# New planned durations and priorities for the attention part of an attention and two-MoE kernel

## The chip, the cores and the metric

The kernel runs on one core of a Trainium2 chip. The metric is the device time of one execution in microseconds (us); three runs of the kernel before gave 1052.19, 1050.07 and 1051.02, median 1051.02 us. PE is TensorE, DVE is VectorE, ACT is ScalarE, POOL is GpSimd and SP is the engine that issues the DMAs here.

## The reference

Inputs are q, k, v of shape (4, 8, 576, 64), a memory M of (4, 8, 64, 64) with a normaliser z of (4, 8, 64), and one gate beta per head. Per head:

```
local = softmax(causal(q k^T / 8)) v
q_p   = phi(q)                  # phi(x) = x + 1 for x > 0, else exp(x)
mem   = (q_p M) / (q_p . z + 1e-6)
out   = g mem + (1 - g) local   # g = sigmoid(beta)
```

The result, seen as 2304 tokens of 512 values, goes through two feed-forward layers (512 to 2048 to 512): `(mish(x w_in)) w_out`, and then the same with silu and a second pair of weights. The weights arrive as 64-bit floats.

## The kernel before, in words

**Attention.** The 32 heads are done as 16 pairs; a pair's two heads stand side by side in the 128 partitions. The operations of one pair are listed with their planned engine, duration and dependencies in `pair_steps()`. Their names: `ld*` loads; `phe`, `phu`, `phf` make phi(q) (two halves on ACT, the joining on DVE), `phz`, `phr`, `pha`, `phd`, `phg`, `phm` its normalised form (POOL and DVE); `Tk`, `Tq`, `Tp`, `Ts`, `Tr` are PE transposes and `Tkh`, `Tqh`, ... their copies out of PSUM (`Ts` and `Tr` are the 64-row remainder; `Tsqh` and `Tsph` are two small copies each on DVE, `Tph` two on ACT). For query blocks 4 to 0: scores `s` on PE, masking with the row extreme `r` on DVE, exponential with row sum `e` on ACT, then `a` (POOL), `d` (DVE, reciprocal) and the normalisation `n` (POOL). `X1` to `X6` and `Xs` transpose the normalised probabilities on PE, `X1h` and so on copy them to the tiles h and W (odd numbers on ACT, even ones on DVE; `X1h` and `X5h` are three copies), `Vhi` and `Vlo` multiply by V and M on PE, and `Vhic`, `Vloc` copy the result to xT.

**Weights.** Each of the 64 jobs of a weight block (two layers, 16 blocks, two parts) is loaded, decoded from 64-bit to 32-bit floats in five DVE steps (`abs`, `b0` to `b3`, lines 757 to 772), rounded on ACT (`hi`, line 780), and the rest is formed on POOL (`lo`, line 784). Eight jobs fit in beside attention; two more can be decoded and then wait. There are two raw buffers and one for the value.

**MoE.** Tokens come in six blocks of 384, the 2048 inner values in four groups of four blocks. A unit is `in` (12 matmuls, lines 838 to 840), the activation and its split (lines 853 to 855), and `out` (matmuls of line 875). Its input is split into xh and xl (lines 821 and 824). The steps `open0` and `open1` swap the memory of attention's "early" and "late" pools for that of the MoE: `open0` waits for the loads, phi, T, s, r and e steps of the last two pairs, and xh waits for it; the first `out` waits for `open1`, which needs the rest of attention.

**What sets the order.** A planner (`Steps.plan`) replays all operations with their planned durations on five engines, with ring buffers counted; an engine that is free takes, of the operations that are ready, the one with the smallest `late`. That is the due time less the longest planned way to it; pairs fall due one PERIOD apart, and a table SHIFT then adds a number to `late` for every kind of operation (key `('a', name)` for all pairs, `('W', step)` for all weight jobs, `('x', 'h')` and `('x', 'l')` for the input split of the first MoE):

```
for k, x in self.shift.items():
    late[k] += x
```

The order in which the replay starts the operations is the order in which they are written to the engines' queues; the hardware runs each queue in that order, with semaphores between. So a planned duration or a shift has no effect on any instruction, only on the order. The planner's `act(n)` is 0.051 + n/1200 us, `dve(n)` 0.066 + n/960.

Of the kernel before, what the change touches and what calls it, by code (L numbers as in the profile page):

```python
# [202 lines left out]
P = 128  # L203
B, H, S, D = 4, 8, 576, 64
# [7 lines left out]
def width(i):  # L212
    return ST + P * i


def mm(n, k=1):
    return k * max(0.109, n / 2215)


def act(n, ps=True, ptr=0):  # L220
    return (0.051 if ps else 0.093) + n / 1200 + 0.093 * ptr


def dve(n):
    return 0.066 + n / 960
# [26 lines left out]
def pair_steps():  # L252
    m = Pair()
    E = m.place
    for nm, d in (("nk", 1.6), ("nq", 1.7), ("nv", 3.1)):
        E("ld" + nm, "S", d, [], 2.7)
    E("phe", "A", act(640, False), ["ldnq"])
    E("phu", "A", act(640, False), ["ldnq"])
    m.group("t", ("Tk", "P", 0.44, ["ldnk"]), [("Tkh", "A", act(512), ["Tk"])])
    E("phf", "D", dve(640), ["phe", "phu"])  # L260
    m.group("t", ("Tq", "P", 0.44, ["ldnq"]), [("Tqh", "D", dve(512), ["Tq"])])
    E("phz", "G", 1.5, ["phf"])
    E("phr", "D", dve(640), ["phz"])
    E("pha", "G", 0.297, ["phr"])
    E("phd", "D", 0.13, ["pha"])
    E("phg", "G", 0.17, ["phd"])
    E("phm", "G", 1.23, ["phg"])
    m.group("t", ("Ts", "P", 0.11, ["ldnk", "ldnq"]),
            [("Tskh", "A", act(128), ["Ts"]), ("Tsqh", "D", 0.27, ["Ts"])])
    m.group("t", ("Tr", "P", 0.06, ["phm"]),  # L270
            [("Tsph", "D", 0.27, ["Tr"])])
    qk = ["Tkh", "Tqh", "Tskh", "Tsqh"]
    for i in (4, 3, 2, 1):
        for x in range(2 if i == 4 else 1):
            n = SA if i == 4 else width(i)
            E(f"s4{x}" if i == 4 else f"s{i}", "P", mm(n, 4), qk)
        for j in range(2):
            w = width(i)
            if i == 4:
                for x in range(2):  # L280
                    E(f"r4{j}{x}", "D", dve(SA) + 0.067 * x, [f"s4{x}"] + ([f"r4{j}0"] if x else []), 0.17)
                    m.uses.append(("s", f"s4{x}{j}", [f"s4{x}"], [f"r4{j}{x}"]))
                dep = [f"r4{j}1"]
            else:
                E(f"r{i}{j}", "D", dve(w), [f"s{i}"], 0.17)
                m.uses.append(("s", f"s{i}{j}", [f"s{i}"], [f"r{i}{j}"]))
                dep = [f"r{i}{j}"]
            E(f"e{i}{j}", "A", act(w, False, 2), dep)
            r = f"r4{j}0" if i == 4 else f"r{i}{j}"
            m.uses.append(("sm", r, [r], [f"e{i}{j}"]))  # L290
        E(f"a{i}", "G", 0.273, [f"e{i}0", f"e{i}1"])
        E(f"d{i}", "D", 0.08, [f"a{i}"])
        for j in range(2):
            E(f"n{i}{j}", "G", 0.327 + width(i) / 1200, [f"d{i}"])
        if i == 3:
            m.group("t", ("Tp", "P", 0.44, ["phm"]), [("Tph", "A", 2 * act(512), ["Tp"])])
        if i == 1:
            m.group("s", ("s0", "P", 0.25, qk), [("r00", "D", dve(ST), ["s0"], 0.17)])
            E("e00", "A", act(ST, False, 2), ["r00"])
            m.uses.append(("sm", "r00", ["r00"], ["e00"]))  # L300
            E("a0", "G", 0.273, ["e00"])
            E("d0", "D", 0.08, ["a0"])
            E("n00", "G", 0.434, ["d0"])

        def X(g, deps):
            m.group("t", (f"X{g}", "P", 0.44, deps),
                    [(f"X{g}h", "A", 3 * act(256) if g in (1, 5) else act(512), [f"X{g}"]) if g % 2 else (f"X{g}h", "D", dve(512), [f"X{g}"])])

        def V(half, groups):
            w = S - HI0 if half == "hi" else HI0  # L310
            n = f"V{half}"
            m.group("x", (n, "P", 1.99 if half == "hi" else 1.29, ["Tph", "ldnv", "Tsph"] + [f"X{g}h" for g in groups]),
                    [(n + "c", "A", act(w), [n])])
        if i == 2:
            hi = [f"n{x}{j}" for x in (3, 4) for j in range(2)]
            for g in (1, 2, 3, 4):
                X(g, hi)
            V("hi", (1, 2, 3, 4))
        if i == 1:
            lo = [f"n{x}{j}" for x in (1, 2) for j in range(2)]  # L320
            X(5, lo)
            m.group("t", ("Xs", "P", 0.11, ["n00"]), [("Xsh", "D", 0.45, ["Xs"])])
            X(6, lo)
            V("lo", (5, 6, "s"))
    for n, (e, d, _, _) in m.ops.items():
        if e == "P":
            i = n[1:2]
            m.cols[n] = {
                "s": lambda: (192, 192) if n == "s0" else [3 * (SA if i == "4" else width(int(i)))] * 2,
                "V": lambda: (4608, 4608) if n == "Vhi" else (2816, 2816),  # L330
                "X": lambda: (256, 256) if n == "Xs" else (1024, 1024),
                "T": lambda: (256, 128) if n == "Ts" else (128, 64) if n == "Tr" else (1024, 1024)}[n[0]]()
    return m
# [384 lines left out]
GC = NF // NG  # L718
# [5 lines left out]
class Weights:  # L724
# [64 lines left out]
    def register(self, m, due, last):  # L789

        m.cap.update({"W.raw": 2, "W.val": self.VALS})
        for n, job in enumerate(self.jobs):
            ph, i, part = job
            f = self.steps(n)
            k = i % SLOTS
            ring = f"W.{k}{part}"
            m.cap[ring] = 1
            J = lambda x: ("W", job, x)
            t = due(job)
            for x, e, d, deps in (("ld", "S", 3.8, []), ("abs", "D", 0.465, ["ld"]), ("b0", "D", 0.465, ["abs"]),  # L800
                                  ("b1", "D", 0.465, ["b0"]), ("b2", "D", 0.735, ["b1"]), ("b3", "D", 0.78, ["b2"]),
                                  ("hi", "A", 0.57, ["b3"] + (["open1"] if k >= GC else [])),
                                  ("lo", "G", 1.38, ["hi"])):
                m.add(J(x), e, d, [y if y == "open1" else J(y) for y in deps], f[x], t)
            m.hold("W.raw", job, [J("ld")], [J("lo")], order=n)
            m.hold("W.val", job, [J("abs")], [J("b3")], order=n)
            m.hold(ring, job, [J("hi")], last(job), order=n)


class Moe:  # L810
# [185 lines left out]
        self.w.register(m, wdue, wlast)  # L996


PERIOD = 12.53
SHIFT = {  # L1000
# [16 lines left out]
}  # L1017


# [22 lines left out]
def kernel(  # L1042
# [6 lines left out]
    weights = Weights(tc, ctx, [(moe_w_in, moe_w_out), (moe2_w_in, moe2_w_out)])  # L1049
    attn = Attn(tc, xT, q, k, v, M_prev, z_prev, beta, PERIOD)  # L1050
    attn.consts()
# [43 lines left out]
```

## Time and profile before

| | us |
|---|---|
| median of three runs | 1051.02 |
| the profiled execution | 1052.46 |
| its span, first to last instruction | 1050.7 |
| PE busy | 1017.0 (97%), 5824 matmuls |
| DVE busy | 557.5 (53%) |
| ACT busy | 460.2 (44%) |
| POOL busy | 311.1 (30%) |

Busy shares are averages over two unlike parts: attention, up to about 245 us, with all engines at work, and the two MoE layers, in which PE works nearly without a break. Idle time of an engine costs time only where the end hangs on it. An engine's waits are put down to the one that came last. Where one operation starts before the one ahead of it has quite ended, the sum of their durations is a little more than the busy time.

### The profile page before, as it was taken

The page shows a single profiled execution, that of the slowest core. Times are in us where ns is not written, and L with a number is a line of the kernel's source. Part 1 is how long each engine was busy: PE and PEld are TensorE (multiplying, and loading weights), DVE is VectorE, ACT ScalarE, POOL GpSimd, SP SyncE. Part 2 cuts the span into 40 slices and gives each one's busy share as a digit, 9 for nine tenths or more (in the row PEclk, how much of TensorE's full clock was granted, in tenths as well). Part 3 has the DMA queues.
Part 4 walks back from the last instruction along what each step waited for, and adds up shares of the span by engine and source line. Part 5 has one row for each costly group of instructions (what it writes and reads, how often), then busy time and mean ns, then how long its engine had stood idle before and what let it go on. Part 6 is the DMA issues. An engine that isn't in the chain of part 4 may idle for free.

```text
span 1050.7 us, 15745 instructions
## 1 busy us (share of the span) xinstructions
PE 1017.0 (97%) x5824; PEld 903.2 (86%) x5824; DVE 557.5 (53%) x1286; ACT 460.2 (44%) x1071; POOL 311.1 (30%) x413
## 2 busy tenths in 40 slices
PE   6989888989999999999999999999999999999998
PEld 4655555659999999999999999899989999999897
DVE  6999999773743732573278338511752372212222
ACT  6887878887333422332234334423422232222221
POOL 6878897779211200220023325100200120000000
PEclk9999999999999999999999999999999999999999
DMA  5533443200311300220022003200310120000011
GB/s 134 134 91 92 106 103 89 48 14 1 120 42 43 98 21 1 81 81 1 1 82 80 1 3 98 61 1 21 101 40 1 41 81 1 1 1 31 31 61 61
DMA packets 85309, 55.03 MB, mean 52 GB/s; under 512 B 61936, under 2 KB 78320, under 8 KB 85232
## 3 DMA queue, kind: packets, MB, share of 16 engines
q1 hardware_dynamic: 85232, 54.02, 18.2%
q8 instruction: 46, 0.75, 0.3%
q14 instruction: 31, 0.25, 0.1%
HBM read 49.29 MB, written 4.72 MB: 51 GB/s over the span
## 4 chain that ended last, share of the span: by engine, by line
PE 85%; DVE 6%; POOL 4%; ACT 3%; issue 1%; DMA 1%; SPq 0%; POOLq 0%; ACTq 0%; DVEq 0%
PE acc L875 38%; PE hp L838 13%; PE hp L839 13%; PE hp L840 13%; PE ps_s L567 3%; POOL P L599 2%; PE ps_x L672 2%; PE ps_t L636 2%; DVE sm L560 2%; ACT P L584 1%; DVE h L482 1%; ACT W L479 1%; PE ps_t L487 1%; POOL z L614 1%; POOL P L617 0%
## 5 line engine op out<-in xcount | busy, mean ns | idle before, releaser
L853 ACT ACTIVATE a<-hp 128x384 f32<-128x384 f32 x192 | 94.4, 491 | 477.8 <-PE hp L840 477.7
L855 DVE TENSOR_TENSOR gl<-a,gh 128x384 fp32r<-128x384 f32 x192 | 115.4, 602 | 333.3 <-ACT gh L854 333.2
L838 PE MATMUL hp<-xh,w 128*128 128x384 f32 x768 | 259.1, 337 | 0.0
L839 PE MATMUL hp<-xl,w 128*128 128x384 f32 x768 | 258.5, 337 | 0.4 <-POOL xl L824 0.4
L840 PE MATMUL hp<-xh,w 128*128 128x384 f32 x768 | 258.5, 337 | 0.0
L784 POOL TENSOR_TENSOR w<-stg,w 128x512 fp32r<-128x512 f32 x64 | 85.2, 1333 | 471.6 <-ACT w L780 342.8
L875 PE MATMUL acc<-gh,w 128*128 128x384 f32 x768 | 211.8, 337 | 0.0
L875 PE MATMUL acc<-w,gh 128*128 128x512 f32 x576 | 180.4, 394 | 0.0
L839 PEld LDWEIGHTS hp<-xl,w 128*128 128x128 f32 x768 | 144.2, 188 | 4.6 <-POOL xl L824 0.6
L838 PEld LDWEIGHTS hp<-xh,w 128*128 128x128 f32 x768 | 144.2, 188 | 4.5 <-issue 0.3
L840 PEld LDWEIGHTS hp<-xh,w 128*128 128x128 f32 x768 | 144.2, 188 | 0.0
L875 PEld LDWEIGHTS acc<-gh,w 128*128 128x128 f32 x768 | 140.6, 188 | 0.0
L875 PE MATMUL acc<-gl,w 128*128 128x384 f32 x384 | 129.2, 337 | 0.0
L875 PEld LDWEIGHTS acc<-w,gh 128*128 128x128 f32 x576 | 106.9, 188 | 17.4
L892 DVE TENSOR_TENSOR xT<-acc,xT 128x384 f32<-128x384 f32 (+1 forms) x126 | 74.1, 613 | 84.4 <-PE acc L875 84.4
L875 PE MATMUL acc<-w,gl 128*128 128x512 f32 x288 | 113.8, 395 | 0.2 <-DVE gl L855 0.2
L854 ACT CAST gh<-a 128x384 fp32r<-128x384 f32 x192 | 98.6, 514 | 5.9 <-PE acc L875 0.4
L599 POOL TENSOR_SCALAR P<-P,z,g 128x448 f32<-128x448 f32 (+3 forms) x128 | 92.4, 731 | 9.3 <-DVE z L616 7.0
L584 ACT ACTIVATE P<-sm,m 128x448 f32<-128x448 f32 (+4 forms) x144 | 83.4, 582 | 15.1 <-DVE m L560 13.2
L875 PEld LDWEIGHTS acc<-gl,w 128*128 128x128 f32 x384 | 72.1, 188 | 0.0
L636 PE MATMUL ps_t<-ident,P 128*128 128x128 f32 x384 | 57.6, 285 | 9.3 <-POOL P L599 3.7
L636 PEld LDWEIGHTS ps_t<-ident,P 128*128 128x128 f32 x384 | 42.0, 143 | 28.6 <-POOL P L599 7.2
(79 smaller groups left out, 1111.6 us busy)
## 6 DMA issues: line engine op xcount, KB each, us to landing
stg<-in_moe_w_in_dram SPq DMA_DIRECT2D x32, 512.0 KB, 3.7
stg<-in_moe_w_out_dram SPq DMA_DIRECT2D x32, 512.0 KB, 3.5
out_dram<-xT SPq DMA_DIRECT2D x18, 256.0 KB, 2.0
nq<-in_q_dram SPq DMA_DIRECT2D x32, 128.0 KB, 2.7
nk<-in_k_dram SPq DMA_DIRECT2D x32, 128.0 KB, 2.7
nv<-in_v_dram SPq DMA_DIRECT2D x32, 128.0 KB, 2.5
z<-in_z_prev_dram SPq DMA_DIRECT2D x4, 256.0 KB, 4.4
nq<-in_q_dram SPq DMA_DIRECT2D x16, 32.0 KB, 2.5
```

The source lines that it names most:

```text
L584: nc.scalar.activation(G(f"P{i}")[:, 1 - j if i else 1], s[f"sm{i}{j}"], AF.Exp, bias=s[f"m{i}"][:, j:j + 1], scale=-1.0, accum_out=G(f"z{ ...
L599: f[f"n{i}{j}"] = lambda i=i, j=j: nc.gpsimd.tensor_scalar(s[f"P{i}"][:, 1 - j], s[f"P{i}"][:, 1 - j], s[f"z{i}"][:, j:j + 1], self.g1[:, ...
L636: nc.tensor.transpose(ps[:, o:o + P], src, self.ident)
L784: nc.gpsimd.tensor_tensor(w[:, 1, :], self.raw[job][:, :, 0].bitcast(F32), w[:, 0, :].bitcast(F32), op=ALU.subtract)
L838: nc.tensor.matmul(hp, lhsT=wh, rhs=xh, start=(kc == 0), stop=False)
L839: nc.tensor.matmul(hp, lhsT=wh, rhs=xl, start=False, stop=False)
L840: nc.tensor.matmul(hp, lhsT=wl, rhs=xh, start=False, stop=(kc == KC - 1))
L853: f["si"] = lambda: nc.scalar.activation(self.new(u, "a", TB), self.hp[u], fn)
L854: f["gh"] = lambda: nc.scalar.copy(self.new(u, "gh", TB, F32R), g("a"))
L855: f["gl"] = lambda: nc.vector.tensor_tensor(self.new(u, "gl", TB, F32R), g("a"), g("gh").bitcast(F32), op=ALU.subtract)
L875: nc.tensor.matmul(o, lhsT=a, rhs=b, start=(first and k == 0), stop=(last and k == 2))
L892: nc.vector.tensor_tensor(part, acc, part, op=ALU.add)
```

## The change

Planned durations of `phz`, `phg`, `phm`, `Tsqh`, `Tsph`, `Tph`, `X1h`, `X5h`, the normalisations and the five decoding steps of the first eight weight jobs are raised; PERIOD goes from 12.53 to 12.920, and the table SHIFT is replaced (it now also has entries for weights and for xh).

```diff
-    E("phz", "G", 1.5, ["phf"])
+    E("phz", "G", 1.57, ["phf"])
-    E("phg", "G", 0.17, ["phd"])
-    E("phm", "G", 1.23, ["phg"])
+    E("phg", "G", 0.23, ["phd"])
+    E("phm", "G", 1.28, ["phg"])
-            [("Tskh", "A", act(128), ["Ts"]), ("Tsqh", "D", 0.27, ["Ts"])])
+            [("Tskh", "A", act(128), ["Ts"]), ("Tsqh", "D", 0.48, ["Ts"])])
-            [("Tsph", "D", 0.27, ["Tr"])])
+            [("Tsph", "D", 0.48, ["Tr"])])
-            E(f"n{i}{j}", "G", 0.327 + width(i) / 1200, [f"d{i}"])
+            E(f"n{i}{j}", "G", 0.387 + width(i) / 1200, [f"d{i}"])
-            m.group("t", ("Tp", "P", 0.44, ["phm"]), [("Tph", "A", 2 * act(512), ["Tp"])])
+            m.group("t", ("Tp", "P", 0.44, ["phm"]), [("Tph", "A", 1.18, ["Tp"])])
-            E("n00", "G", 0.434, ["d0"])
+            E("n00", "G", 0.5, ["d0"])
-                    [(f"X{g}h", "A", 3 * act(256) if g in (1, 5) else act(512), ...
+                    [(f"X{g}h", "A", 0.91 if g in (1, 5) else act(512), ...
+            slow = 0.2 if ph == 0 and i < GC else 0.0
-                m.add(J(x), e, d, [y if y == "open1" else J(y) for y in deps], f[x], t)
+                m.add(J(x), e, d + (slow if e == "D" else 0.0), [y if y == "open1" else J(y) for y in deps], f[x], t)
-PERIOD = 12.53
+PERIOD = 12.920
```

Entries of SHIFT that the text speaks of, old and new:

```
Tk   18.22   32.27     Tq    7.80   25.99     phu  52.49   63.70
Vhi  47.28  184.28     X3h -13.04 -163.92     X5h  -9.48 -150.25
r401 -0.45 -144.61     r410 -13.59 -153.95    e40  -0.27 -110.98
s3    none  -55.00     Vlo  -6.28  -91.80     x l   2.55   11.88
W ld  none   54.80     W abs none  -30.37     W b0  none  -22.37
W b1  none  -29.57     W b2  none   -3.04     W b3  none   -6.91
W hi  none   -2.90     W lo  none   -9.09     x h   none   -1.87
```

## Rows read from the trace of the kernel before

**Rows 1.** Busy time of each engine by stage; columns in the first line.

```profile
core 0: us, PE busy (x) PEld busy (x) DVE busy (x) ACT busy (x) POOL busy (x), PEclk, DMA share, GB/s
0.00:20.00 20.00, 11.82 (x60) 7.92 (x61) 12.16 (x46) 11.80 (x30) 10.57 (x26) 1.00 0.58 135
...
25.00:100.00 75.00, 68.10 (x481) 43.12 (x481) 71.34 (x234) 60.80 (x170) 62.42 (x97) 0.98 0.45 112
100.00:175.00 75.00, 66.51 (x500) 43.50 (x497) 70.29 (x228) 63.04 (x180) 61.70 (x95) 1.00 0.42 100
175.00:235.00 60.00, 54.11 (x397) 36.13 (x397) 44.05 (x171) 50.14 (x147) 47.28 (x84) 0.97 0.16 36
...
241.00:1000.00 759.00, 758.83 (x4099) 722.70 (x4098) 340.74 (x568) 252.77 (x500) 118.52 (x97) 1.00 0.13 41
1000.00:1050.70 50.70, 46.99 (x233) 41.73 (x231) 11.81 (x20) 11.05 (x22) 0.00 (x0) 0.98 0.15 57
```

**Rows 2.** PE's waits before 241 us: total, times, longest (us).

```profile
PE ps_t L487 <- DMA nq<-in_q_dram: 4.3, 1, 4.3
PE ps_t L636 <- POOL P L599: 3.7, 6, 1.1
PE ps_t L487 <- DVE h L482: 2.9, 2, 1.9
...
PE ps_t L542 <- POOL e L520: 2.1, 2, 1.6
PE ps_t L653 <- POOL P L617: 1.7, 2, 1.1
PE ps_t L636 <- DVE qT L482: 1.6, 1, 1.6
PE ps_t L636 <- DVE h L482: 1.5, 3, 0.9
...
PE ps_t L487 <- ACT h L479: 0.7, 2, 0.3
...
PE ps_t L636 <- ACT h L479: 0.6, 1, 0.6
```

**Rows 3.** POOL's groups, 20 to 241 us: count, busy us, mean ns, idle before.

```profile
L599 POOL TENSOR_SCALAR P<-P,z,g 128x576 f32<-128x576 f32 x31 | 28.2, 915 | 2.5 <-DVE z L616 2.1
...
L520 POOL TENSOR_TENSOR e<-e,c 128x640 f32<-128x640 f32 x15 | 18.9, 1258 | 0.8
...
L617 POOL TENSOR_SCALAR P<-P,z,g1s 128x128 f32<-128x128 f32 x16 | 9.1, 566 | 2.1 <-DVE z L616 2.1
```

**Rows 4.** ACT's groups, 20 to 241 us: the copies of Tph.

```profile
L479 ACT COPY W<-ps_t 64x512 f32<-64x512 f32 x30 | 17.4, 579 | 0.4 <-PE ps_t L487 0.2
```

**Rows 5.** DVE's groups, 25 to 175 us: the half copies to W.

```profile
L482 DVE COPY W<-ps_t 64x64 f32<-64x64 f32 x40 | 8.8, 220 | 0.6
```

**Rows 6.** The five decoding steps by stage: DVE busy (count), clock, DMA share, GB/s.

```profile
25.00:100.00 75.00, 18.09 (x25) 0.98 0.45 112
100.00:175.00 75.00, 19.18 (x25) 1.00 0.42 100
175.00:235.00 60.00, 0.00 (x0) 0.97 0.16 36
```

**Rows 7.** The first decoding step, whole execution: ns min/median/max, first and last start.

```profile
L757 DVE TENSOR_SCALAR val<-stg x64: 414/428/1184, 28.2 to 861.2; 128x512 uint32<-128x512 uint32 x64
```

**Rows 8.** One stretch of 10 us by the columns of rows 1.

```profile
200.00:210.00 10.00, 7.93 (x52) 5.47 (x51) 6.07 (x20) 8.29 (x25) 8.12 (x15) 0.83 0.15 34
```

**Rows 9.** Timeline at the end of attention: start us, us, instruction, [idle before].

```profile
232.20 3.40 ACT L821 CAST xh<-xT 128x384 fp32r<-128x384 f32 x8
...
234.58 0.42 PE L838 MATMUL hp<-xh,w 128*128 128x384 f32 x1
...
245.30 1.68 PE L672 MATMUL ps_x<-h,nv 128*64 128x256 f32 x16
```

More of the change, by code (lines that the diff above doesn't have):

```diff
@@ L302, in pair_steps @@
             E("d0", "D", 0.08, ["a0"])
-            E("n00", "G", 0.434, ["d0"])
+            E("n00", "G", 0.5, ["d0"])
         def X(g, deps):
             m.group("t", (f"X{g}", "P", 0.44, deps),
-                    [(f"X{g}h", "A", 3 * act(256) if g in (1, 5) else act(512), [f"X{g}"]) if g % 2 else (f"X{g}h", "D", dve(512), [f"X{g}"])])
+                    [(f"X{g}h", "A", 0.91 if g in (1, 5) else act(512), [f"X{g}"]) if g % 2 else (f"X{g}h", "D", dve(512), [f"X{g}"])])
         def V(half, groups):
```

35 rows, old and new, of the table SHIFT are left out of this document.

## The prediction

> **What bounds the kernel now.** I read the stage table first, then the list of what TensorE waited for, then per-engine groups. The table [rows 1] splits the span of 1050.70 us into a part in which PE never stops and a part in which it does: from 241 to 1000 us PE is busy 758.83 of 759.00 us (the two MoE phases), while in the attention part it is idle 8.18 us before 20, then 75.00 - 68.10 = 6.90, 75.00 - 66.51 = 8.49 and 60.00 - 54.11 = 5.89 us, together 21.28 us between 25 and 235. The last 3.71 us of idle are the output's drain. The change issues the same matmuls, so the time is PE's work plus PE's idle time, and only those 21.28 us (and the 8.18 of the start, whose main piece is the first DMA, 4.3 us [rows 2]) can move. The reader should also see in rows 1 that no other engine leaves much room there: DVE is busy 71.34 and 70.29 of each 75 us, ACT and POOL 61 to 63, and that DVE's load falls to 44.05 of 60 after 175.
>
> The list of waits [rows 2] says who ended PE's idle moments. None is long (the longest of each kind is 0.3 to 1.9 us after the first loads), none repeats in every one of 16 pairs. This is a stage of many near-misses between five in-order queues, whose order a planner wrote; it isn't one chain that a shorter instruction would cut.
>
> **The change, part by part.** No instruction, tile or buffer changes; what changes is numbers of the planner, and so the order of each queue.
>
> *Normalisation, phm, n00 on POOL.* The planner had 0.807 us for the 576-wide normalisation (0.327 + 576/1200), 1.23 for phm, 0.434 for n00; it now has 0.867, 1.28 and 0.50. The trace has 0.915, 1.258 and 0.566 [rows 3]. So POOL ran later than planned by 0.108 us per normalisation, eight in a pair, and the new figure takes up 0.06 of it. PE waits released by these operations: 3.7 (P L599) + 2.1 (e L520) + 1.7 (P L617) = 7.5 us [rows 2]. The right cost makes nothing shorter; it lets the planner put other ready work in front of the transposes that wait. Below, nothing is recovered, or as much is lost (+7.5) if the new order meets as many late normalisations again; above, all 7.5. The new figures close about half of the gap (0.06 of 0.108), so I take half: -3.75.
>
> *Copies on ACT.* Tph was planned at 0.955 and is now 1.18; the trace has 2 x 0.579 = 1.16 [rows 4]. The three copies behind X1 and X5 go from 0.793 to 0.91. PE's waits released by ACT's copies to h: 0.7 + 0.6 = 1.3 us [rows 2]. Bounds -1.3 to +1.3, half taken: -0.65.
>
> *Copies and decoding on DVE.* The pairs of half copies (Tsqh, Tsph) go from 0.27 to 0.48; the trace has 2 x 0.220 = 0.44 [rows 5]. A decoding step was planned at 2.91 / 5 = 0.582 us and is now 0.782 for the first eight jobs; the trace shows (18.09 + 19.18) / 50 = 0.745 before 175 us [rows 6]. Behind a decoding step stand DVE's copies h and qT, and PE waited 2.9 + 1.5 + 1.6 = 6.0 us for these [rows 2]. The copies' own planned cost stays as it is, so only the part of the lateness that comes from decoding is repaired: a quarter, -1.5; bounds -6.0 to +6.0.
>
> One row speaks against a fixed 0.2: the first decoding step lasts 0.414 us at least, 0.428 in the median of all 64 and 1.184 at most [rows 7]. The Trainium skill (SBUF — State Buffer, "Who interferes with whom") says why such a spread can come: GpSimd and VectorE share a pair of ports, and whoever has it locks the other out for a whole instruction. By that rule a decoding step's length hangs on what POOL does beside it, so a new order brings new lengths, and the -1.5 would be 0. The forecast would then be 1047.7 where the row's mean gives 1046.2.
>
> *Priorities and period.* A shift moves one kind of operation in its queue, for all 16 pairs. Many of the new values are saturated: Vhi goes from +47 to +184, but both are over two periods of 12.5 to 12.9, and the tiles that Vhi frees have two buffers, so it was last in line already. Likewise X3h, X5h, r401 and r410 at -145 to -164 simply go first. Steps that open a pair become less urgent (Tk +18 to +32, Tq +8 to +26, phu +52 to +64). I can't derive the new queues by hand; any reshuffle also makes waits of its own. Bounds: the stage's idle could vanish (-21.3), or run everywhere at the rate of a poor stretch, 10.00 - 7.93 = 2.07 us in 10 [rows 8], which over 210 us is 43.5, so +22. I take one more wait of the usual longest size, POOL's 1.1 [rows 2]: +1.1, since most of the shifts point the same way as before.
>
> *Weights.* Job loads become later by 54.8 on SP's queue, past the loads of up to four pairs; the first two raw buffers are waited for by DVE only. All ten jobs that fit were decoded before 175 us [rows 6], and the MoE needs the first at about 235, so 60 us cover it; without that cover one late job is its five steps, 3.7 us. In the MoE, PE was short by 0.17 us in 759 [rows 1] with DVE busy 340.74: DVE's slack hides moved steps there, so 0, with +3.7 for a job that comes late.
>
> **Sum.** -3.75 - 0.65 - 1.5 + 1.1 = -4.8 us. The profiled execution took 1052.46 us (span 1050.70 and 1.76 around it); it becomes 1047.7. It lies 1.44 above the median of the runs shown, 1051.02, so the forecast for the median is 1046.2.
>
> **Rivals.**
>
> *The waits only move.* DVE is busy 141.6 of 150 us between 25 and 175 [rows 1], and no order shortens that; if DVE's queue sets the pace of this stage, PE's 15.4 us of idle there are its slack and a recovered POOL wait turns up as one on a copy. For it: DVE at 95%. Against it: from 175 to 235 DVE is at 73%, yet PE is idle at the same rate (5.89 in 60), so DVE's load doesn't explain the idle time. The DVE lengths that depend on their neighbours raise its chance. Time: 1051.0, with 1.5 either way.
>
> *Slower: the tail loses its filler.* MoE work may start only when the steps of the last two pairs that use the early pool are done. In the trace xh starts at 232.20, the first matmul of the MoE at 234.58, the last V of attention at 245.30 [rows 9]: for 11 us PE has both to choose from, and stops nowhere. If the pairs open later (Tk, Tq, phu), the last early step can come after the last V's transposes. Then PE pays the way from xh to the first matmul, 234.58 - 232.20 = 2.4, the last pair alone for about 12 us at 2.07 in 10, 2.5, and 1.7 for a fall of the granted clock as in 200 to 210 (0.83 of 10 us) [rows 8], 6.6 in all. The same late opening leaves PE short of work in the middle, so nothing is recovered: 1051.0 + 6.6 = 1057.6. It decides where xh starts less than 2.4 us before the last V ends. For it: every opening step of Tk, Tq, phu is shifted later; against it: scores and first halves (s3, r401, r410, e40) go first, and these end the early pool.
>
> *Decoding moves behind 175.* DVE has 60.00 - 44.05 = 15.95 us free from 175 to 235 and does no decoding there [rows 1, 6]. Decoding is what the planner fits in where DVE is free; with 1.0 us more per job, fewer fit early. Three jobs moved, 3 x 3.73 = 11.2 us out of the stage where DVE is at 95%, give 1051.0 - 11.2 = 1039.8. Against it: abs, b0 and b1 are shifted 22 to 30 earlier, and the longer period makes attention's due times later against the weights'.
>
> **How the numbers follow.** Forecast 0.45 (1042 to 1049.5 by its own), waits that move 0.24, tail 0.18, decoding moved 0.13. A difference below 0.2% (2.1 us) can't be told from none here. Faster: 0.13 and nearly all of the forecast's, 0.57; same: the moving waits and the forecast's rim, 0.24; slower: the tail and a little of the moving waits, 0.19. The range leaves out less than half of the tail rival and a little of the decoding one: 1038 to 1057.
>
> **What would show it.** Right: PE's idle time between 25 and 235 falls from 21.3 to some 16.5 us; the waits on P and e released by POOL fall from 7.5 to about 4; 241 to 1000 stays without idle time; xh again starts some 10 us before the last V starts. Wrong: POOL's waits shrink while those on h and qT grow by as much (the waits moved); xh starts within 2.4 us of the last V (the tail); decoding steps between 175 and 235 (the third rival); or idle time of PE in the MoE, which none of the cases has.

## The result and the profile after

The changed kernel takes 1041.37 us (median of 4, 1040.10 to 1041.92), the kernel before 1051.01 in the same runs: a ratio of 0.9901, interval 0.9889 to 0.9913. It is 9.6 us faster, twice what was forecast (4.8 us). In a later set of runs on one chip it had 1040.22 against 1051.93 (0.9886, 0.9869 to 0.9902).

The stage table of the changed kernel, in the columns of [rows 1], its profiled execution taking 1041.53 us:

```profile
0.00:20.00 20.00, 12.68 (x50) 7.86 (x50) 9.65 (x38) 9.46 (x22) 8.63 (x25) 1.00 0.54 125
...
25.00:100.00 75.00, 70.64 (x526) 46.04 (x524) 72.20 (x246) 68.42 (x190) 67.78 (x110) 1.00 0.46 113
100.00:175.00 75.00, 72.41 (x544) 47.59 (x543) 70.99 (x255) 68.74 (x197) 66.41 (x107) 1.00 0.37 85
175.00:235.00 60.00, 55.97 (x399) 38.55 (x395) 45.22 (x146) 50.59 (x139) 55.80 (x79) 0.97 0.21 53
...
241.00:1000.00 759.00, 758.24 (x4077) 722.60 (x4076) 342.02 (x568) 245.60 (x483) 107.52 (x86) 1.00 0.13 41
```

PE's idle time between 25 and 235 us is 4.36 + 2.59 + 4.03 = 10.98 us, against 21.28 before: 10.3 of the 11.3 us by which the span shrank (1050.7 to 1039.4). DVE is no less busy up to 175 us (143.2 of 150; before 141.6), and ACT and POOL are busier (137.2 against 123.8, 134.2 against 124.1): in the same time every engine gets more of attention done.

PE's waits before 241 us, as in [rows 2]: total, times, longest:

```profile
PE ps_t L487 <- DMA nq<-in_q_dram: 4.3, 1, 4.3
PE ps_t L636 <- POOL P L599: 4.0, 6, 1.2
...
PE ps_t L487 <- ACT h L479: 1.9, 4, 1.0
PE ps_t L542 <- POOL e L520: 1.5, 2, 0.8
PE ps_t L636 <- DVE h L482: 1.1, 3, 0.5
PE ps_s L567 <- ACT kT L479: 0.7, 1, 0.7
PE ps_s L605 <- DVE m L560: 0.5, 1, 0.5
```

The five decoding steps by stage, as in [rows 6]:

```profile
25.00:100.00 75.00, 14.01 (x17) 1.00 0.46 113
100.00:175.00 75.00, 10.46 (x16) 1.00 0.37 85
175.00:235.00 60.00, 12.50 (x18) 0.97 0.21 53
```

Of the fifty steps 17 now begin behind 175 us, and one straddles it (it is counted on both sides); before it was none. The end of attention, as in [rows 9], keeps its shape: xh first at 218.82, the first matmul of the MoE at 227.26, attention's last V from 229.10.

```profile
218.82 1.34 ACT L822 CAST xh<-xT 128x384 fp32r<-128x384 f32 x3
...
227.26 0.44 PE L839 MATMUL hp<-xh,w 128*128 128x384 f32 x1
...
229.10 0.82 PE L672 MATMUL ps_x<-h,nv 128*64 128x256 f32 x8
```

By these tables the third rival (decoding moves behind 175 us, 1039.8) looks right in mechanism and in size. The experiments were made to see whether it is.

### The profile page after: what moved, and what is told of

Its sections match the earlier page's. It is cut to its first block, busy times and chain, and to the rows that moved or that the text cites. A ratio compares the mean times of both kernels' runs of the same rounds, so it can differ in the third digit from the quotient of the medians.

```text
span 1039.4 us, 15745 instructions
## 1 busy us (share of the span) xinstructions
PE 1016.7 (98%) x5824; PEld 903.2 (87%) x5824; DVE 556.9 (54%) x1286; ACT 460.9 (44%) x1071; POOL 316.1 (30%) x413
## 4 chain that ended last, share of the span: by engine, by line
PE 74%; DVE 2%; DMA 1%; POOL 1%; issue 0%; ACT 0%; DVEq 0%
PE acc L876 37%; PE hp L839 12%; PE hp L841 12%; PE hp L840 12%; DMA stg<-in_moe_w_in_dram 1%; DVE val L765 1%; PE ps_x L672 0%; POOL w L784 0%; DVE xT L893 0%; DMA stg<-in_moe_w_out_dram 0%; DVE val L757 0%; DVE val L769 0%; DVE val L767 0%; ACT w L780 0%; DVE gl L856 0%
## 5 line engine op out<-in xcount | busy, mean ns | idle before, releaser
L599 POOL TENSOR_SCALAR P<-P,z,g 128x192 f32<-128x192 f32 (+3 forms) x128 | 94.1, 743 | 6.8 <-DVE z L616 3.9
L584 ACT ACTIVATE P<-sm,m 128x576 f32<-128x576 f32 (+4 forms) x144 | 83.6, 583 | 7.7 <-DVE m L560 7.2
L780 ACT CAST w<-stg 128x512 fp32r<-128x512 f32 x64 | 42.2, 660 | 56.3 <-DVE stg L772 49.7
L876 PEld LDWEIGHTS acc<-w,gl 128*128 128x128 f32 x288 | 54.1, 188 | 14.6 <-DVE gl L856 2.0
```

What stands on the lines that cost most here:

```text
L584: nc.scalar.activation(G(f"P{i}")[:, 1 - j if i else 1], s[f"sm{i}{j}"], AF.Exp, bias=s[f"m{i}"][:, j:j + 1], scale=-1.0, accum_out=G(f"z{ ...
L599: f[f"n{i}{j}"] = lambda i=i, j=j: nc.gpsimd.tensor_scalar(s[f"P{i}"][:, 1 - j], s[f"P{i}"][:, 1 - j], s[f"z{i}"][:, j:j + 1], self.g1[:, ...
L780: nc.scalar.copy(w[:, 0, :], self.raw[job][:, :, 0].bitcast(F32))
L876: nc.tensor.matmul(o, lhsT=a, rhs=b, start=(first and k == 0), stop=(last and k == 2))
```

## The experiments

**Theories.** A: the place of decoding carries the gain, since DVE sets the pace up to 175 us. B: the order as a whole carries it, and that order fits only the numbers with which it was sought. C and F: the truer durations carry it. D (and D'): any decoding step less on DVE helps. E: it doesn't, since round trips between the queues set the pace. G: the large shifts carry it.

**Decoding's places alone, both ways.** Each file keeps one kernel's queues and sets the ten jobs' steps (load to lo) at the places which they have in the other's, counted in operations of the same queue that stand ahead.

```diff
-    for k in self.plan():
+    for k in moved(self, self.plan()):     # SPOTS[job, step] = operations ahead of it
```

> Attention's queues and all planned numbers are those of the kernel before; only the ten weight jobs that are handled beside attention have their eight steps (load, five decoding steps, hi, lo) set at the places that they have in the changed kernel's queues, so that 18 of the 50 decoding steps come after 175 us instead of none. Theory A, the place of decoding carries the gain (DVE sets the pace up to about 175 us, and 12.8 us of decoding leave that stage): 1040 to 1044 us, PE's idle time between 25 and 235 falls from 21.3 to 10 to 13 us. Theory B, the new order of attention as a whole carries it (fewer near-misses between the queues): 1048 to 1054 us, idle time 18 to 24, since a moved step stands ahead of operations that the plan had not put behind one.

> The mirror image: attention's queues of the changed kernel, with the ten jobs' steps at the places of the kernel before, so that no decoding stands behind about 175 us. Theory A: most of the 9.6 us is lost, 1048 to 1053 us, and DVE is again 94% busy up to 175 and under 80% after. Theory B: most is kept, 1041 to 1045 us, with PE's idle time between 25 and 235 at 11 to 15 us.

Measured: 1066.64 (ratio 1.0153, 1.0132 to 1.0174) and 1069.63 (1.0174, 1.0155 to 1.0193). Neither theory had that: both mixtures are 16 to 19 us slower than the kernel before. Stage rows of late decoding:

```profile
25.00:100.00 75.00, 66.79 (x469) 42.30 (x469) 64.28 (x217) 57.63 (x164) 57.50 (x94) 0.98 0.41 98
100.00:175.00 75.00, 66.96 (x493) 43.93 (x491) 60.60 (x217) 62.28 (x177) 56.78 (x92) 1.00 0.37 87
175.00:235.00 60.00, 51.37 (x360) 33.83 (x356) 48.80 (x174) 44.36 (x129) 49.99 (x77) 0.96 0.27 69
```

DVE is relieved up to 175 us (64.28 and 60.60 of 75, before 71.34 and 70.29), and attention is slower: PE is idle 24.9 us between 25 and 235 (before 21.3) and 3.3 between 235 and 1000 (before 0.55), and its busy time over the whole execution is 7.9 us longer. So DVE's busy share alone is not what bounds it: moving decoding late is not enough, and theory A falls as it stood. What the reader should see is a pair of waits from 25 to 235 us, first in the kernel before, then with late decoding:

```profile
POOL P L599 <- DVE z L616: 6.5, 16, 1.0
DVE z L616 <- POOL z L614: 7.3, 12, 1.8
```

```profile
POOL P L599 <- DVE z L616: 14.0, 16, 2.0
DVE z L616 <- POOL z L614: 12.3, 13, 2.6
```

POOL's normalisation waits for DVE's reciprocal, and DVE for POOL's sum, about twice as long as before. The trace shows one way in which this comes about. Three decoding steps in a row fill DVE's queue for 3.6 us, and POOL then waits 1.97 us for a reciprocal that stands behind them:

```profile
118.45 0.80 DVE L767 TENSOR_SCALAR val<-val 128x512 uint32<-128x512 uint32 x1
...
120.41 1.63 DVE L772 SCALAR_TENSOR_TENSOR stg<-stg,val 128x512 uint32<-128x512 uint32 x1
...
126.20 0.16 DVE L616 RECIPROCAL z<-z 128x2 f32<-128x2 f32 x1
```

```profile
126.54 1.21 POOL L599 TENSOR_SCALAR P<-P,z,g 128x320 f32<-128x320 f32 x2 [1.97 <-DVE z L616]
```

How many of the other waits come from decoding is not shown; at two other long ones (POOL at 98.76 and 113.47 us) mostly copies and maskings stand just ahead of the reciprocal.

The mirror image shows a second loss, in two neighbouring stretches (columns of [rows 1]):

```profile
80.00:84.00 4.00, 1.43 (x9) 0.92 (x11) 2.20 (x13) 0.99 (x4) 1.65 (x4) 0.93 0.41 107
84.00:88.00 4.00, 4.00 (x27) 2.65 (x24) 3.46 (x10) 1.89 (x6) 3.39 (x6) 0.64 0.01 3
```

PE waited 3.12 us for POOL's P, and in the stretch after it the granted clock averages 0.64, so most of it ran at the lower of the clock's two levels, 1.2 GHz. PE's busy time over the whole execution is 1031.2 us there and 1017.0 before, for the same matmuls: of the 17.5 us by which its profiled execution is longer, 14.2 are PE's longer busy time and only 3.3 idle time.

**One half of the change at a time.** New durations with the old PERIOD and SHIFT, and the reverse:

> The new planned durations with the old PERIOD and SHIFT, planned anew. Theory C, the durations make the plan fit the chip: at least half of the gain, 1041 to 1046 us. Theory A: the longer decoding steps push decoding later (some steps after 175 us), and the time falls by as much as leaves the first stage, about 0.7 us for each step after 175. Theory B, an order that a search found and that only its own numbers give: no gain, 1047 to 1057.

> The new PERIOD and SHIFT with the old planned durations, planned anew. Theory A: decoding with the old short durations is done by 175 us or so, hence no gain, 1048 to 1053 us. Theory B in the form that the priorities are what counts: 1041 to 1046 us. Theory C: no gain or a loss, 1048 to 1058 us.

Measured: 1048.25 (0.9973, 0.9962 to 0.9984) and 1050.31 (0.9992, 0.9983 to 1.0002). The durations alone give a quarter of the gain, the priorities alone none that can be told from noise; 2.7 and 0.8 thousandths don't add up to 9.9. With the durations alone 7 of 50 steps came behind 175 us, where A's price would be 5 us; 2.4 came.

**One number taken back, or put in.** The 0.2 us per decoding step, taken out of the changed kernel, and put alone into the kernel before; and 0.16 in its place, the trace's own mean:

```diff
-            slow = 0.2 if ph == 0 and i < GC else 0.0
+            slow = 0.0 if ph == 0 and i < GC else 0.0      # the third run: 0.16
```

> The changed kernel without the 0.2 us that were added to each planned decoding step of the first eight jobs, planned anew; all other new durations, PERIOD and SHIFT stay. Theory B, the priorities fit only the durations that they were sought with: all of the gain goes, 1046 to 1055 us, by waits of all kinds. Theory F, the decoding cost is what repaired DVE's copies (PE's waits for h and qT fell from 6.0 to 1.1 us): the waits for h and qT come back to 4 us or more and the time to 1045 to 1049, the other waits stay. Neither: 1040 to 1044.

> The kernel before with only the 0.2 us for each decoding step of the first eight jobs, planned anew with the old SHIFT and PERIOD. Theory F: PE's waits for h and qT fall from 6.0 to 3 us or less and the time to 1045 to 1049 us. Theory B: the same as before or worse, 1048 to 1058 us. The durations together gave 1048.25.

> The changed kernel with 0.16 instead of 0.2 us added to each decoding step, planned anew. 0.582 + 0.16 is 0.742 us, what the trace of the kernel before shows as the mean (0.745), so the planned cost is nearer to the chip's. Theory F, it is the truth of the cost that pays: 1040 to 1043 us. Theory B, the priorities fit one set of numbers only and any other order that comes out of them is an unsought one: 1046 to 1056 us.

Measured: 1053.35 (1.0029, 1.0013 to 1.0044), 1055.28 (1.0040, 1.0026 to 1.0054) and 1056.46 (1.0033, 1.0018 to 1.0048). The third varies most, from 1051.73 to 1058.38 in ten runs. Theory F falls: the truest cost gives a slower kernel than the rounder one, and the number that takes all of the gain away when it is missing costs 4.7 us when it stands alone. PE's waits for h and qT in the first of them are 2.1 + 0.7 + 0.3 = 3.1 us, not the 4 that F wanted. This is what B expects: these are other orders, which nobody sought.

These runs also answer theory A where the planner itself made the order. The decoding steps behind 175 us, with 0.2 alone and with 0.16, as in [rows 6]:

```profile
175.00:235.00 60.00, 6.43 (x8) 1.00 0.19 43
```

```profile
175.00:235.00 60.00, 6.91 (x9) 1.00 0.19 44
```

Eight and nine steps came late, and both kernels are slower than the one before, which has none there. But the changed kernel and the other kernels of its speed, which follow, have twelve or more, so these runs don't take apart an order that is good and one that is late in decoding as well.

**Small moves of all priorities.** Every entry of SHIFT off by up to 0.3 us, two draws:

```diff
-    ('a', 'd3'): 3.93, ('a', 'n30'): 19.28, ('a', 'n31'): 13.76, ('a', 'Tp'): 44.74, ('a', 'Tph'): -1.3,
+    ('a', 'd3'): 3.77, ('a', 'n30'): 19.12, ('a', 'n31'): 13.59, ('a', 'Tp'): 44.72, ('a', 'Tph'): -1.43,
```

> The changed kernel with every entry of SHIFT moved by a random amount of at most 0.3 us (entries run from -164 to +184), durations and PERIOD unchanged, planned anew. Theory B: a fraction of a microsecond in the priorities gives another order, which nobody sought, and several microseconds of the gain go: 1044 to 1054 us, spread over many small waits. Theory G, the large shifts (which steps go first and which last) carry the gain: 1040 to 1043 us.

> As the run before with another draw of the random amounts. Theory B: 1044 to 1054 us and not the same as the other draw. Theory G: 1040 to 1043 us.

Measured: 1044.31 (0.9927, 0.9913 to 0.9940) and 1043.65 (0.9920, 0.9907 to 0.9934), against a kernel before at 1052.47 here; the changed kernel has 0.9901. So about three quarters of the gain stay, between B and G. Where PE's queue first differs from the changed kernel's does not explain it: of attention's 320 operations on PE the first 271 are the same in the second draw and only 68 in the first, and the two can't be told apart; without the 0.2 it is 32, with 0.16 it is 34. The stage rows of the second draw:

```profile
25.00:100.00 75.00, 70.69 (x524) 45.67 (x520) 72.01 (x245) 68.33 (x189) 68.70 (x109) 1.00 0.45 112
100.00:175.00 75.00, 72.19 (x541) 47.68 (x542) 70.98 (x256) 68.57 (x197) 66.23 (x109) 1.00 0.37 85
175.00:235.00 60.00, 54.38 (x392) 36.57 (x393) 47.45 (x147) 49.28 (x135) 54.45 (x78) 0.97 0.21 55
```

Up to 175 us PE's idle time is that of the changed kernel (7.12 against 6.95 us); behind the place where the queues part it is 5.62 against 4.03. Without the 0.2 the stages of 150 and 60 us have 12.5 and 3.4 us of idle time, a granted clock of 0.98 and 0.97, and PE is busy 1024.8 us in all; its profiled execution, 1056.76 us, is the longest of five.

The planner's own replay sees part of this without the chip. The planned end, worked out by replaying the planner that each kernel file holds, is 1016.4 us for the kernel before and 1011.1 for the changed one. With the same durations it is 1012.4 for the second draw, 1017.0 for the first and 1020.6 with the old PERIOD and SHIFT, and the chip has these four in the same order (0.9901, 0.9920, 0.9927, 0.9973; only the two draws can't be told apart). Without the 0.2 and with 0.16 it is 1020.4 and 1022.0, and both are slow. It fails for the priorities alone (planned 1012.4, no gain on the chip) and for the held jobs further down (planned 1011.1, yet 3.2 us faster than the changed kernel). So an order that nobody sought is mostly one that the planner itself rates as longer; its figure ranks, but does not give, the time.

**Less decoding, nothing else moved.** Ten jobs' five steps replaced by one:

> The changed kernel with the five decoding steps of the first ten weight jobs replaced by one (a bitwise and from the high to the low word), so the weights of these jobs are not those of the reference: what is left out is abs, b0, b1, b2 and the second operand of b3. All else keeps its place. It takes some 31 of 37 us of DVE out of attention. Theory D: DVE's load sets the pace, 1020 to 1030 us. Theory E, round trips and POOL or ACT (91% busy each) set it as soon as DVE is relieved: 1033 to 1040 us.

Measured: 1032.10 (0.9823, 0.9809 to 0.9838), 0.8% below the changed kernel's ratio. Removing some 31 us of DVE's work gives 8 us; PE's idle time between 25 and 235 is 4.6 us. The time lies between the ranges of D and E: inside this order, decoding costs about a quarter of its length. At that rate the 12.8 us of decoding that the change took out of the stage before 175 us would be worth at most 3.4 of the 9.6 us (an estimate from this run).

**Two jobs behind attention.** The ninth and tenth jobs feed the second group of blocks only. First by hand, in two forms:

```diff
+SPOTS = {(8, step): 419, (9, step): 419}     # all ten steps ahead of the first gl
+SPOTS = {(8, step): 419, (9, step): 423}     # the tenth job behind the fourth gl; its hi and lo later
```

> The changed kernel with one thing moved: the five decoding steps of the ninth and tenth weight job, which only the second group of MoE blocks needs, stand behind all of attention's operations in DVE's queue, ahead of the first gl. Nothing else changes its place. These ten steps took 7.5 us of DVE before 225 us. Theory D, taking a decoding step out of a queue that is in lockstep always helps because everything behind it comes earlier: 1037 to 1040 us. Theory E, the pace at the end of attention is set by round trips between the queues and not by DVE's load: 1040.5 to 1042.5 us, no change.

> As the run with two jobs behind attention, but only the ninth job's decoding stands ahead of the first gl; the tenth job's stands behind the fourth gl, where DVE was idle for 4.9 us, and its hi and lo follow later. In the run before, PE's waits released by P fell from 4.0 to 2.4 and those by h by 0.6 us, and PE then waited 3.3 us for the first gl, which ten decoding steps of 1.1 to 1.4 us each (beside POOL's xl) had held up. Theory D', the relief is real and was given back by that wait: 1038 to 1040 us, no wait for gl. Theory E, no relief: 1041 to 1042.5 us.

Measured: 1041.72 (0.9918, 0.9903 to 0.9933) and 1044.46 (0.9928, 0.9914 to 0.9941): no faster than the changed kernel, which is what E expects of the first. But the rows say why. Waits of PE in the first form, and its DVE rows with POOL's beside them (start us, us):

```profile
PE acc L876 <- DVE gl L856: 3.3, 1, 3.3
...
PE ps_t L636 <- POOL P L599: 2.4, 5, 0.7
```

```profile
222.03 0.42 DVE L757 TENSOR_SCALAR val<-stg 128x512 uint32<-128x512 uint32 x1
222.49 0.43 DVE L765 TENSOR_SCALAR val<-val 128x512 f32<-128x512 f32 x1
222.95 1.12 DVE L767 TENSOR_SCALAR val<-val 128x512 uint32<-128x512 uint32 x1
...
226.94 1.12 DVE L757 TENSOR_SCALAR val<-stg 128x512 uint32<-128x512 uint32 x1
```

```profile
222.69 17.18 POOL L825 TENSOR_TENSOR xl<-xT,xh 128x384 fp32r<-128x384 f32 x14 [1.07 <-issue]
```

The waits on P fell from 4.0 to 2.4 us, and the block of decoding then held up the first gl by 3.3. In the second form another gl came 4.0 us late, and the granted clock behind that wait averaged 0.69:

```profile
250.16 0.69 PE L876 MATMUL acc<-gl,w 128*128 128x384 f32 x1 [4.03 <-DVE gl L856]
```

```profile
250.00:260.00 10.00, 9.84 (x41) 9.84 (x42) 6.56 (x13) 3.12 (x6) 2.62 (x2) 0.69 0.35 113
```

A relief given back is not the same as no relief. So the planner was told to hold the two jobs until 208 and until 232 (or 240) of its own time, and to reckon 0.5 us more for each of their steps:

```diff
-            slow = 0.2 if ph == 0 and i < GC else 0.0
+            slow = 0.2 if ph == 0 and i < GC else 0.5 if n < 10 else 0.0
+            held = {8: 208, 9: 232}.get(n, 0.0)
-                m.add(J(x), e, d + (slow if e == "D" else 0.0), [...], f[x], t)
+                m.add(J(x), e, d + (slow if e == "D" else 0.0), [...], f[x], t, held if x == "abs" else 0.0)
```

> The changed kernel in which the planner may begin the ninth job's decoding only behind attention's last DVE operations and the tenth job's only behind the fifth gl, with 0.5 us added to the planned steps of both; everything of attention up to the ninth job keeps its order. In the two runs that moved these jobs by hand, attention's idle time fell by about 1.6 us but a gl came 3.3 and 4.0 us late behind five decoding steps. Theory D', the relief is real once no gl stands behind a block of decoding: 1037 to 1040 us on a chip where the changed kernel has 1041.4, PE's idle time between 25 and 235 at 9 to 10 us and none for gl. Theory E: no faster than the changed kernel in this call.

> As the run before, with the tenth job's decoding begun one MoE unit and a half later. Theory D': the same time as the run before within 1 us, since attention's queues are the same in both and the weights of this job are needed only by the second group of blocks. If it is slower, the weights' chain has become the bound.

> The changed kernel itself, unaltered, for a comparison on the same chip: 0.9889 to 0.9913 of the kernel before.

Measured on one chip: 1037.06 (0.9857, 0.9842 to 0.9871), 1036.92 (the same ratio) and, for the changed kernel, 1040.22 (0.9886). The relief is real and worth 3.2 us, and these two versions beat both kernels. The last stage of the changed kernel beside it, then that of the first version, and the first version's waits on P:

```profile
175.00:235.00 60.00, 55.96 (x410) 39.42 (x407) 46.48 (x148) 52.19 (x143) 56.39 (x80) 1.00 0.20 53
```

```profile
175.00:235.00 60.00, 57.96 (x420) 41.20 (x417) 45.79 (x142) 54.16 (x148) 55.51 (x79) 1.00 0.20 52
```

```profile
PE ps_t L636 <- POOL P L599: 2.4, 5, 0.7
```

PE's idle time in this stage is 2.04 us, against 4.04 in the changed kernel; the tenth job's steps now stand in ones to threes between the gl, and PE's idle time from 235 to 1000 is 0.14 us, against 0.82.

## Why the prediction was wrong

- **Where the time is** was right: PE's idle time in attention, 21.3 us of it open to an order; 241 to 1000 us stayed nearly without gaps (0.17 and 0.76 us), and only the order moved it. The identity "PE's work plus PE's idle time" held for this pair (1017.0 and 1016.7 us busy); the two mixtures show that it is no law, since PE's busy time is 8 and 14 us longer in them, at a lower granted clock.
- **POOL's retimed operations**, -3.75: the waits on P, e and P L617 went from 7.5 to 5.5, so -2.0. Half of them was too much; P L599 itself went up, from 3.7 to 4.0.
- **ACT's copies**, -0.65: 1.3 to 1.9, so +0.6.
- **DVE's copies**, -1.5: the waits on h and qT went from 6.0 to 1.1, so -4.9, the largest miss among the retimed operations. That the longer planned decoding did it is not shown: put alone into the kernel before, it made the kernel slower.
- **Priorities**, +1.1 for one more wait: the step that failed. "Most of the shifts point the same way as before" was taken to mean an order about as good as the old one. All the waits that the prediction didn't name (z, xT, m, c, the small ones on h, qT, kT and W) went from 7.5 to 2.6 us, so -4.9 in place of +1.1, the largest miss of the four terms. The four sum to -11.2 in the lists of waits, against -11.3 of span: they say which waits shrank, not which edit did it.
- **Adding up shares by releaser** was the fault beneath it. Each term took the waits that one retimed kind of operation releases and gave the edit a share of them. But the two halves of the change alone are worth 2.4 and 0.4 us and both together 9.6, one duration less turns the gain into a loss, and the closest duration to the trace does worse than a rounder one. No part of the change has a price that holds without the others; the order that came out has one.
- **The third rival** had the time (1039.8 against 1041.4) and the visible sign, and was still not the cause as it was put: with decoding late and the old queues the kernel takes 1066.6. What holds of it is that decoding that no queue waits behind is worth having out of attention: 3.2 us for two jobs.
- **The tail** kept its filler (xh 10 us ahead of the last V), as forecast; "waits only move" was wrong, since DVE at 95% went on at 95% with 12.8 us less decoding and more attention in the same 150 us.
- **Decoding's changing lengths** were weighed rightly: its first step took 0.42 us with POOL idle and 1.12 beside xl, and the mean of the fifty steps was 0.74 us in the changed kernel (before 0.745), but 0.65 in the mirror image and 0.82 without the 0.2. The Trainium skill (SBUF — State Buffer, "Who interferes with whom") states that whoever of VectorE and GpSimd has the shared ports first blocks the other for a whole instruction; the longer steps beside xl agree with it. That these lengths cost the forecast's sum anything is not shown.

Left open: what in the order carries the gain. The runs show that neither half of the change, nor the place of decoding alone, nor the truer cost of decoding does. Whether the order gains by being late in decoding and good elsewhere at once, and whether it is more than the best of many that a search tried, was not separated.

## What to carry to other kernels

When a change re-seeds a planner or a search, price the stage's whole idle time as one quantity with a wide range: here each of four shares by releaser was wrong, and two halves worth 2.4 and 0.4 us made 9.6 together. Look at what the planner's own replay says of the new order, but don't take it for the time. Then test an order as a whole: places of decoding moved alone into the other order cost 16 us and more. Where filler work stands in a queue that is in lockstep with others, move what isn't needed yet behind the stage, one piece between two urgent operations, and check what is late next: here ten steps in a block held up a gl by 3.3 us, and with five of them spread between later gl 3.2 us were kept.

## What the runs showed of the hardware

The same DVE instruction of 128x512 elements took 0.42 us with POOL between two instructions and 1.12 us a few microseconds later beside POOL's xl. Not every instruction there is longer: three gl of the changed kernel that ran beside xl took 1.06, 1.30 and 0.56 us.

Two waits of PE, of 3.12 and 4.03 us, were followed by granted clocks of 0.64 and 0.69 over the next 4 and 10 us, so such a wait can cost twice, once as idle time and once as slower matmuls. Its length alone doesn't decide it. The wait of 3.3 us for the first gl was followed by full clock:

```profile
235.00:240.00 5.00, 5.00 (x30) 5.00 (x29) 2.04 (x2) 0.94 (x2) 5.00 (x6) 1.00 0.00 0
```

And in the mirror image the clock stood at 0.50 from 58 to 66 us after three waits of 0.46 to 1.09 us between 53 and 58, in which time PE was busy 2.88 of 5 us.
